# Attention and feed-forward kernel: lam fetched as one packet and spread over the partitions by a matmul, q and k first in SyncE's queue, one activation table for Ln and Exp, and a new order table for all engines

## The chip, the cores and the metric

One core of a Trainium2 chip runs the whole program. The metric is the time of one execution on the device in microseconds, as the median of several runs. Names of the engines: PE is TensorE (PEld its weight loads), DVE VectorE, ACT ScalarE, POOL GpSimd, SP SyncE, which here only starts DMAs. ACT and POOL start some DMAs too.

## The reference

Two steps, all inputs and the output in float32. The first is attention with a decay lam per head (batch 4, 8 heads, 768 positions, head size 64), in blocks of 64 positions with a running state. The second takes its result as 3072 tokens of 512 and puts them through two matrix products with a sine between them.

```python
rel = pos[:, None] - pos[None, :]
Dmask = np.where(rel >= 0, lam ** rel, 0.0)              # per head
for b in range(nb):                                      # blocks of 64 positions
    intra = (qb @ kb.T * Dmask) @ vb
    inter = (qb * lam ** (pos + 1)) @ kv_state
    out[b] = intra + inter
    kv_state = lam ** 64 * kv_state + (kb * lam ** (63 - pos)).T @ vb
x = out.transpose(0, 2, 1, 3).reshape(3072, 512)
h = x @ w_in                                             # 512 x 2048
g = h + np.sin(alpha * h) ** 2 / (alpha + 1e-9)
out = g @ w_out                                          # 2048 x 512
```

## The kernel before

**Attention** works on 24 blocks of 128 tokens (six to each batch). lam never enters a mask: q is multiplied by powers of lam (`Lq`), k by negative powers (`Lp` for the first four blocks, `Lk` for the rest), so that the scores need only a mask of zeros and ones. The powers are exp of n ln(lam): the exponents `E_f` come from iotas, `lnlam` is Ln of lam (L438), `lnL` the product of both (L441), and four exponentials (L443 to L449) make `Lq`, `Lp` and `Lk`. A block then goes: scaling of q and k on DVE or POOL (L468, L478, L485, L497), a cast of v (L491, L500), transposes on PE with copies to SBUF, scores (L618) and their masking into `Sm` on DVE (L629), the state `Z` (L654) with its casts `Zd` or `Zc` on ACT or DVE, and the output (L700 to L722; the first four blocks use L765 and L785), which is cast into `xT`, the transposed input of the feed-forward part (L732, L745).

**The feed-forward part** works on six chunks of 512 tokens. `unit_A` is 128 of the 2048 columns of h for 512 tokens: four matmuls into one PSUM bank (L828), the sine on ACT (L838), its square on ACT or POOL (L842, L843), and the sum with h on DVE (L845), which gives `gT` and frees the bank. `unit_A2` is the same work for two times 128 columns and half the tokens (L862 to L880). `unit_B` is the second product for chunk 0 (L893), with a copy to `osb` (L907) and stores on ACT's queue (L913). Chunks 1 to 5 do the second product in a form with seven products instead of eight (`unit_P`, L981). It needs five sums of quarters of w2 for each of two halves of w2, made once (`weight_sums`, L936, ten operations on DVE or POOL; three of each five go into other buffers, two are made in place in `w2`), and sums of `gT` for each chunk (`token_sums`, L959, on POOL or DVE). `finish` puts the products together (L1003 to L1027).

**The order.** `_Plan` collects about 1050 operations with what they read and write. A table, `ORDER`, holds for each engine the numbers of its operations in the order in which it issues them; where an operation may run on more than one engine, the table that lists its number decides. `emit` adds the semaphore waits. Each engine works through its list strictly in order: what waits holds all that stands behind it. DMAs are operations in these lists as well (`load`, L324), so a DMA holds its place on SP, ACT or POOL. Pairs in PE's table, such as (64, 128), are 64 filler matmuls of 128 columns on a buffer of ones (`spin`, L1140) that keep PE running while nothing else is ready.

**The start.** lam was loaded with a DMA that writes the same eight numbers to all 128 partitions (128 packets of 32 bytes), first in SP's queue, followed by k and q of the first four blocks, their v, and `ws`, the first 512 columns of w1 in float32, which ACT casts in two halves (L393). ACT loads three tables of functions: one for Ln (L438), one for Exp (brought in by a small operation, L440) and one for Sin (L450).

## Time and profile before

| | |
|---|---|
| time, median of 3 runs | 210.52 us (209.93 to 210.64) |
| profiled execution | 209.95 us |
| its span (first to last instruction) | 208.2 us |
| busy: PE, DVE, ACT, POOL | 200.0, 168.5, 147.7, 132.4 us |
| first matmul of the feed-forward part | 19.04 us after the span's start |
| granted TensorE clock | 1.00 from 19.2 to 180 us |

All times of the profile are microseconds from the start of the span. A row of the timeline gives start, duration, engine, line and operation, and in brackets the idle time ahead of it with what ended it. A row of the stretches gives its bounds, its length, PE's busy time with the number of instructions, the granted clock (1.00 is full), the share of the DMA engines and GB/s. A row of the DMA issues ends with KB and the median time from issue to landing.

### The profile page before, as it was taken

The numbers are of one execution on the slowest core, as the hardware profiler recorded it, in microseconds if no ns is written. First come the engines' busy times: TensorE is split into PE (matmuls) and PEld (weight loads), VectorE is DVE, ScalarE is ACT, GpSimd is POOL, SyncE is SP. The second block draws the span as 40 slices with busy tenths as digits, with TensorE's granted clock in tenths as the row PEclk, the third lists the DMA queues.
The fourth block names the chain that finished last, engine by engine and source line by source line (L and its number), as shares of the span: only waits on it lengthen the run. The fifth ranks groups of instructions, "written<-read, shape, count | busy, mean of one in ns | idle before, by whom it ended". The sixth has DMA issues, their size and how long they took to land.

```text
span 208.2 us, 4897 instructions
## 1 busy us (share of the span) xinstructions
PE 200.0 (96%) x1972; PEld 136.8 (66%) x1972; DVE 168.5 (81%) x296; ACT 147.7 (71%) x270; POOL 132.4 (64%) x140
## 2 busy tenths in 40 slices
PE   6988999999997999998999999999999999999995
PEld 6756444557765877665657576665667666667994
DVE  2898567886989999987988979899798866767854
ACT  5658999448998999976979776898765579734300
POOL 6065689834968987954796850958851695585400
DMA  4999999999899999799997999380300004000324
GB/s 133 323 315 216 202 255 214 213 238 245 197 179 230 232 250 248 154 215 206 208 245 156 242 271 185 67 194 26 136 0 3 0 32 169 3 0 20 128 94 165
DMA packets 83222, 34.40 MB, mean 165 GB/s; under 512 B 59632, under 2 KB 80384, under 8 KB 83200
## 3 DMA queue, kind: packets, MB, share of 16 engines
q1 hardware_dynamic: 78544, 29.24, 62.5%
q0 software_dynamic: 3696, 3.67, 10.9%
q10 hardware_dynamic: 960, 1.19, 1.9%
q8 instruction: 15, 0.25, 0.5%
q14 instruction: 7, 0.06, 0.1%
HBM read 27.28 MB, written 6.29 MB: 161 GB/s over the span
## 4 chain that ended last, share of the span: by engine, by line
PE 79%; DVE 9%; ACT 4%; DMA 3%; SPq 2%; issue 1%; ACTq 1%; POOL 0%
PE bank L828 28%; PE bank L981 26%; PE bank L862 7%; PE bank L893 6%; PE bank L722 3%; PE bank L618 3%; DMA v<-in_v_dram 3%; SPq L324 2%; DVE gT L880 2%; DVE Sm L629 2%; DVE gT L845 2%; PE bank L700 1%; DVE w L936 1%; PE bank L654 1%; ACT Zd L672 1%; PE bank L662 1%
## 5 line engine op out<-in xcount | busy, mean ns | idle before, releaser
L828 PE MATMUL bank<-xT,w 128*128 128x512 bf16 x296 | 70.9, 380 | 1.0 <-ACT kept L1018 0.7
L845 DVE SCALAR_TENSOR_TENSOR gT<-u,rinv,bank 128x512 bf16<-128x512 bf16 x74 | 53.6, 744 | 18.2 <-ACT u L842 14.1
L838 ACT ACTIVATE t<-bank,alpha 128x512 bf16<-128x512 f32 x74 | 49.9, 683 | 19.9 <-PE bank L828 19.0
L828 PEld LDWEIGHTS bank<-xT,w 128*128 128x128 bf16 x296 | 27.8, 98 | 28.8 <-DVE gT L845 1.4
L959 POOL TENSOR_TENSOR gT<-gT 128x512 bf16<-128x512 bf16 x28 | 32.1, 1158 | 14.1 <-DVE Xs L959 8.9
L842 ACT ACTIVATE u<-t 128x512 bf16<-128x512 bf16 x57 | 35.2, 628 | 1.5
L843 POOL TENSOR_TENSOR u<-t 128x512 bf16<-128x512 bf16 x17 | 17.6, 1040 | 25.7 <-ACT t L838 25.7
L629 DVE TENSOR_TENSOR Sm<-bank,mask 128x1024 bf16<-128x1024 f32 x24 | 28.9, 1216 | 3.0 <-PE bank L618 1.1
L862 PE MATMUL bank<-xT,w 128*128 128x256 bf16 x176 | 21.6, 273 | 1.0 <-DVE gT L880 1.0
L880 DVE SCALAR_TENSOR_TENSOR gT<-u,rinv,bank 128x256 bf16<-128x256 bf16 x44 | 18.9, 474 | 4.2 <-ACT u L876 3.5
L959 POOL TENSOR_TENSOR Xs<-gT 128x512 bf16<-128x512 bf16 x19 | 21.8, 1162 | 0.3 <-DVE gT L845 0.3
L981 PE MATMUL bank<-w,gT 128*128 128x256 bf16 (+1 forms) x168 | 20.1, 268 | 0.0
L872 ACT ACTIVATE t<-bank,alpha 128x256 bf16<-128x256 f32 x44 | 18.5, 471 | 2.0 <-PE bank L862 1.7
L981 PE MATMUL bank<-ws,gT 128*128 128x256 bf16 x160 | 19.6, 273 | 0.0
L981 PE MATMUL bank<-w,Xs 128*128 128x256 bf16 (+1 forms) x168 | 19.5, 268 | 0.0
L478 POOL TENSOR_TENSOR qk<-q,Lq 128x512 bf16<-128x512 f32 x17 | 18.2, 1077 | 2.0 <-DMA q<-in_q_dram 2.0
L497 POOL TENSOR_TENSOR qk<-k,Lk 128x512 bf16<-128x512 f32 x16 | 17.4, 1090 | 3.3 <-DMA k<-in_k_dram 3.2
L862 PEld LDWEIGHTS bank<-xT,w 128*128 128x128 bf16 x176 | 16.3, 98 | 4.2 <-DVE gT L880 1.8
L981 PEld LDWEIGHTS bank<-w,gT 128*128 128x128 bf16 x168 | 15.9, 98 | 4.1 <-DVE gT L959 0.2
L981 PEld LDWEIGHTS bank<-w,Xs 128*128 128x128 bf16 x168 | 15.6, 98 | 3.3
L981 PEld LDWEIGHTS bank<-ws,gT 128*128 128x128 bf16 x160 | 15.3, 98 | 3.1 <-ACT xT L732 0.4
L893 PE MATMUL bank<-w,gT 128*128 128x512 bf16 x64 | 15.8, 380 | 0.0
(105 smaller groups left out, 266.0 us busy)
## 6 DMA issues: line engine op xcount, KB each, us to landing
k<-in_k_dram SPq DMA_DIRECT2D x24, 256.0 KB, 5.1
q<-in_q_dram SPq DMA_DIRECT2D x12, 512.0 KB, 6.2
v<-in_v_dram SPq DMA_DIRECT2D x24, 256.0 KB, 5.8
out_dram<-osb SPq DMA_DIRECT2D x18, 256.0 KB, 2.6
w<-in_moe_w_out_dram POOLq DMA_DIRECT2D x4, 512.0 KB, 7.8
w<-in_moe_w_in_dram POOLq DMA_DIRECT2D x3, 512.0 KB, 8.1
ws<-in_moe_w_in_dram SPq DMA_DIRECT2D x2, 512.0 KB, 7.5
out_dram<-osb ACTq DMA_DIRECT2D x8, 128.0 KB, 3.7
```

Source lines behind the costliest of these rows:

```text
L478: lambda e, a=a: e.tensor_tensor(qk2[:, j:j + 2, 4 * a:4 * a + 4, :], q32[:, jq, 4 * a:4 * a + 4, :, :].rearrange("p h t d -> p t h d"), b ...
L629: op("DVE", lambda e: e.tensor_tensor(Sm[js][:, :, :], banks[:, 512 * b0:512 * b0 + 1024].rearrange("p (c i) -> p c i", i=128), bass.AP(ma ...
L828: ins = e.matmul(ps[hb][:, c0:c1], w1[:, kc, 128 * m:128 * (m + 1)], xT[x][:, kc, c0:c1], start=(kc == 0 and c0 == lo), stop=(kc == NKC - ...
L838: op("ACT", lambda e: e.activation(t16[ju][:, w], ps[hb][:, w], ACTF.Sin, scale=alpha[:, m:m + 1]), 0.69 if hi - lo == TCH else 0.475, [ba ...
L842: lambda e: (e.activation(u16[ju][:, w], t16[ju][:, w], ACTF.Square) if e is nc.scalar else e.tensor_tensor(u16[ju][:, w], t16[ju][:, w], ...
L845: op("DVE", lambda e: e.scalar_tensor_tensor(out=gT[g][:, m, w], in0=u16[ju][:, w], scalar=rinv[:, m:m + 1], in1=ps[hb][:, w], op0=ALU.mul ...
L862: ins = e.matmul(ps[hb][:, 256 * i:256 * i + 256], w1[:, kc, 128 * (m + i):128 * (m + i + 1)], xT[x][:, kc, lo:lo + 256], start=(kc == 0 a ...
L872: op("ACT", lambda e, i=i: e.activation(t16[ju][:, 256 * i:256 * i + 256], ps[hb][:, 256 * i:256 * i + 256], ACTF.Sin, scale=alpha[:, m + ...
L880: op("DVE", lambda e, i=i: e.scalar_tensor_tensor(out=gT[g][:, m + i, lo:lo + 256], in0=u16[ju][:, 256 * i:256 * i + 256], scalar=rinv[:, ...
L893: ins = e.matmul(ps[ob][:, w], gT[g][:, m, 128 * s4:128 * (s4 + 1)], w2[:, m, w], start=(m == 0), stop=(m == NM - 1),)
L959: e.tensor_tensor(dst, in0, in1, alu), 0, rd, wr))
L981: ins = e.matmul(ps[ob][:, lo + d0:lo + d1], lhs, rhs[:, d0:d1], start=first and p == 0, stop=(p == NM // 2 - 1), skip_group_check=True)
```

## The change

**lam.** It is loaded as one packet of eight numbers onto partition 0, on ACT's queue, ahead of alpha. Ln works on these eight numbers. A float32 matmul of a row of 128 ones with them writes the result to all 128 partitions of PSUM bank 7, where `lnL` reads it. The memset of the ones is a new DVE operation, the matmul a new PE operation behind the first 24 fillers (before, 64 fillers stood in one row).

**The tables.** ACT asks for one table that holds both Ln and Exp, right behind alpha's DMA. The small Exp operation (L440) is gone, and with it a table load; the Sin table is brought in as before.

```diff
-            load(lam_bc[:, :], bass.AP(lam.tensor, 0, [[0, 128], [1, H]]), "lam", 0.1, "lam", "SP", lat=0.8, runs=1)
-            load(alphaT[:, :], bass.AP(moe_alpha.tensor, 0, [[128, NM], [1, 128]]), "alphaT", 0.1, "alphaT", "ACT", lat=2.0, runs=1)
+            load(lam_sb[:, :], bass.AP(lam.tensor, 0, [[H, 1], [1, H]]), "lam", 0.1, "lam", "ACT", lat=0.8, runs=1)
+            def load_alpha(e):
+                ins = e.dma_start(alphaT[:, :], bass.AP(moe_alpha.tensor, 0, [[128, NM], [1, 128]]))
+                e.preload_act_table_set("natural_log_exp_and_others")
+                return ins
...
-            op("ACT", lambda e: e.activation(lnlam[:, :], lam_bc[:, :], ACTF.Ln), 0.25, ["lam"], ["lnlam"])
-            lnlam_b = bass.AP(lnlam, 0, [[H, 128], [0, 2 * NB + 4], [1, H]])
-            op("ACT", lambda e: e.activation(warm[:, :], lnlam[:, 0:1], ACTF.Exp, scale=0.0), 1.5, ["lnlam"], ["warm"])
+            op("DVE", lambda e: e.memset(ones[:, :], 1.0), 0.1, writes=["ones"])
+            op("ACT", lambda e: e.activation(lnlam[:, :], lam_sb[:, :], ACTF.Ln), 0.25, ["lam"], ["lnlam"])
+            op("PE", lambda e: e.matmul(ps[7][:, 0:H], ones[:, :], lnlam[:, :]), 0.3, ["ones", "lnlam"], [bank(7)])
+            lnlam_b = bass.AP(banks, 512 * 7, [[8 * 512, 128], [0, 2 * NB + 4], [1, H]])
...
-                        wr = [("T", i, x) for x in m] + ([("ws", 256 * (i // 3))] if i < 4 else [] if i == 4 else keys)
+                        wr = [("T", i, x) for x in m] + ([("ws", 0), ("ws", 256)] if i < 4 else [] if i == 4 else keys)
...
         "PE": (
-            (64, 128), 58, (5, 512), 60, 54, (11, 128), 38, 56, 52, 61, 66, 64, (1, 128), 68, 69, 74, 77,
+            (24, 128), 32, (5, 512), (33, 128), 57, 39, 59, 61, 53, 55, 62, (4, 512), 67, 65, 75, 69, 70, 82,
```

The line with `ws` makes the sums that are written into the buffer `ws` wait for both halves of w1's first cast.

**The order table** is new as a whole. The lists keep much of their shape; some 130 operations changed engine. POOL's list now has a scaling of k and one cast of v behind the last k, then a memset of `Zd`, and only then the loads of w1 and w2 (before: the scaling of k, three casts of v, then three loads of w1). The first half of w1's cast has moved from ACT to DVE. DVE has eight of the ten sums of w2 (before seven), POOL two (before three). Three places, line numbers of each kernel's own code:

SP's list at its start; `q32`, `k32`, `v32` are the float32 buffers of q, k and v, `ws` that of w1's first columns. Before:

```order
L324 DMA lam_bc<-in_lam_dram 128x8
L324 DMA k32<-in_k_dram 128x4x128
L324 DMA q32<-in_q_dram 128x4x256
L324 DMA k32<-in_k_dram 128x4x128
L324 DMA q32<-in_q_dram 128x4x256
L324 DMA k32<-in_k_dram 128x4x128 x2
L324 DMA v32<-in_v_dram 128x4x128 x4
```

SP's list at its start, of the changed kernel:

```order
L326 DMA q32<-in_q_dram 128x4x256 x2
L326 DMA k32<-in_k_dram 128x4x128 x2
L326 DMA v32<-in_v_dram 128x4x128
L326 DMA k32<-in_k_dram 128x4x128
L326 DMA v32<-in_v_dram 128x4x128
L326 DMA k32<-in_k_dram 128x4x128
L326 DMA v32<-in_v_dram 128x4x128 x2
```

lam's load is gone from this queue, both q stand ahead of all k, and the last k is now the eighth load, behind two v; it was the sixth data load.

ACT's list at its start, from alpha's load to the Sin table (`warm` is the small buffer of the operations that bring a table in). Before:

```order
L324 DMA alphaT<-in_moe_alpha_dram 16x128
L438 ACT_TABLE_LOAD
L438 ACTIVATE lnlam<-lam_bc 128x8
L440 ACT_TABLE_LOAD
L440 ACTIVATE warm<-lnlam 128x1
L445 ACTIVATE Lp<-lnL 128x32
L449 ACTIVATE Lq<-lnL 128x48
L447 ACTIVATE Lk<-lnL 128x48
L443 ACTIVATE Lq<-lnL 128x32
L450 ACT_TABLE_LOAD
```

ACT's list at the same place, of the changed kernel:

```order
L326 DMA lam_sb<-in_lam_dram 1x8
L409 DMA alphaT<-in_moe_alpha_dram 16x128
L410 ACT_TABLE_LOAD
L447 ACTIVATE lnlam<-lam_sb 1x8
L456 ACTIVATE Lk<-lnL 128x48
L452 ACTIVATE Lq<-lnL 128x32
L454 ACTIVATE Lp<-lnL 128x32
L458 ACTIVATE Lq<-lnL 128x48
L459 ACT_TABLE_LOAD
```

One table load and one operation are gone, lam's load stands here, and the exponentials have another order: `Lk` first, `Lp` third.

DVE's list around the sums of w2 that are made in place, in the first half of chunk 1 (`gT_1` is chunk 1's buffer, `u16` the squared sine, `rinv` 1/alpha, `bank` PSUM). Before:

```order
L936 TENSOR_TENSOR w2<-w2 128x4x256
L880 SCALAR_TENSOR_TENSOR gT_1<-u16_1,rinv,bank 128x256
L880 SCALAR_TENSOR_TENSOR gT_1<-u16_3,rinv,bank 128x256 x2
L880 SCALAR_TENSOR_TENSOR gT_1<-u16_1,rinv,bank 128x256
L936 TENSOR_TENSOR w2<-w2 128x4x256 x2
L880 SCALAR_TENSOR_TENSOR gT_1<-u16_1,rinv,bank 128x256 x2
L629 TENSOR_TENSOR Sm_0<-bank,mask_2 128x1024
```

DVE's list at that place, of the changed kernel:

```order
L945 TENSOR_TENSOR w2<-w2 128x4x256
L889 SCALAR_TENSOR_TENSOR gT_1<-u16_3,rinv,bank 128x256 x2
L889 SCALAR_TENSOR_TENSOR gT_1<-u16_1,rinv,bank 128x256
L916 COPY osb_1<-bank 128x512
L945 TENSOR_TENSOR w2<-w2 128x4x256
L889 SCALAR_TENSOR_TENSOR gT_1<-u16_1,rinv,bank 128x256 x2
L638 TENSOR_TENSOR Sm_0<-bank,mask_2 128x1024
```

Of three sums in place on DVE two are left, and no two stand next to each other; a copy to `osb` stands here now. In ACT's list the two stores of `osb_1` that stood next to each other now stand singly.

More of the change, by code (lines that the diff above doesn't have):

```diff
@@ L293, in bass_lightning_attn__then__act_snake_kernel @@
         identf = sb("identf", [128, 128], F32)
-        lam_bc = sb("lam_bc", [128, H], F32)
-        lnlam = sb("lnlam", [128, H], F32)
+        lam_sb = sb("lam_sb", [1, H], F32)
+        lnlam = sb("lnlam", [1, H], F32)
+        ones = sb("ones", [1, 128], F32)
         E_i = sb("E_i", [128, 2 * NB + 4, H], I32)
@@ L403, in _ @@
             last = {}
-            load(lam_bc[:, :], bass.AP(lam.tensor, 0, [[0, 128], [1, H]]), "lam", 0.1, "lam", "SP", lat=0.8, runs=1)
-            load(alphaT[:, :], bass.AP(moe_alpha.tensor, 0, [[128, NM], [1, 128]]), "alphaT", 0.1, "alphaT", "ACT", lat=2.0, runs=1)
+            load(lam_sb[:, :], bass.AP(lam.tensor, 0, [[H, 1], [1, H]]), "lam", 0.1, "lam", "ACT", lat=0.8, runs=1)
[3 more added lines that the diff above has]
+                return ins
+            op("ACT", load_alpha, 0.1, dma="alphaT", lat=2.0, issue=0.55, runs=1, writes=["alphaT"])
             load_q(0)
```

14 lines of the change are left out of this document (7 added, 7 removed), and 107 rows, old and new, of the table ORDER.

## The prediction

> **What bounds the kernel now.** I read the page first (busy shares and the chain that ended last), then PE's busy time by stretches, then the timeline up to the first matmul of the feed-forward part.
>
> ```profile
> span 208.2 us, 4897 instructions
> PE 200.0 (96%) x1972; PEld 136.8 (66%) x1972; DVE 168.5 (81%) x296; ACT 147.7 (71%) x270; POOL 132.4 (64%) x140
> ...
> DVE  2898567886989999987988979899798866767854
> ...
> PE 79%; DVE 9%; ACT 4%; DMA 3%; SPq 2%; issue 1%; ACTq 1%; POOL 0%
> ...
> 19.20:98.00 78.80, 76.88 (x737) 1.00 1.12 217
> 98.00:180.00 82.00, 81.85 (x720) 1.00 0.55 127
> ...
> 19.04 1.91 PE L862 MATMUL bank<-xT,w 128*128 128x256 bf16 x16
> ```
>
> The reader is to see that TensorE holds 79% of the chain, and that from 98 us to 180 us it is idle for 0.15 us in all. In the row of the stretch from 19.2 us to 98 us it is idle for 78.80 - 76.88 = 1.92 us. The row of digits is VectorE's busy share in 40 slices of 5.2 us each: it is at 90% or more in five slices in a row, from 62 to 88 us. The first row of the feed-forward part (the last line) starts at 19.04 us. The change removes no matmul behind that point, so the end can move for two reasons only: the first such matmul starts at another time, or the 1.92 + 0.15 = 2.07 us of idle time behind it become less or more.
>
> Where those 1.92 us lie is told by two rows of PE's timeline (in brackets the wait ahead of the row and what ended it):
>
> ```profile
> 65.21 1.05 PE L862 MATMUL bank<-xT,w 128*128 128x256 bf16 x8 [0.97 <-DVE gT L880]
> 98.08 1.04 PE L828 MATMUL bank<-xT,w 128*128 128x512 bf16 x4 [0.73 <-ACT kept L1018]
> ```
>
> Together 1.70 of the 1.92 us. The first is the queue of VectorE: the gT that frees the bank stands behind two sums of w2. The last is ScalarE's queue, which had been held while it issued two stores:
>
> ```profile
> 62.24 2.13 DVE L936 TENSOR_TENSOR w<-w 128x1024 bf16<-128x1024 bf16 x2
> 62.22 1.60 POOL L497 TENSOR_TENSOR qk<-k,Lk 128x512 bf16<-128x512 f32 x1
> 93.77 1.66 ACTq L913 DMA_DIRECT2D out_dram<-osb  x2
> ```
>
> **The change, part by part: SyncE's queue.** These are the issues and landings that count (the times behind the sizes are from issue to landing):
>
> ```profile
> 0.81 0.40 SPq L324 DMA_DIRECT2D lam_bc<-in_lam_dram  x1
> 1.25 0.42 SPq L324 DMA_DIRECT2D k<-in_k_dram  x1
> 4.19 0.93 SPq L324 DMA_DIRECT2D k<-in_k_dram  x1
> ...
> k<-in_k_dram SPq DMA_DIRECT2D x1, 256.0 KB, 3.6
> k<-in_k_dram SPq DMA_DIRECT2D x1, 256.0 KB, 6.4
> ...
> 6.35 6.02 DMA v<-in_v_dram
> ...
> 14.53 0.61 POOL L491 CAST v<-v 128x512 bf16<-128x512 f32 x1 [1.50 <-DMA v<-in_v_dram]
> 15.89 0.62 ACT L491 CAST v<-v 128x512 bf16<-128x512 f32 x1
> ```
>
> lam's slot on SyncE goes, so every load behind it is issued 1.25 - 0.81 = 0.44 us earlier. What the stream itself gains lies between nothing (if the transfers and not the issues set the landings) and the 1.05 us between lam's landing (0.81 + 3.0) and the first k's (1.25 + 3.6); I take 0.44, the slot. The first k landed at 4.85, the sixth load (the last k, issued 4.19) at 10.6, the eighth (the second v) at 6.35 + 6.02 = 12.37, and the last v between 14.5, when POOL got the third, and 15.9, when ScalarE cast it. In the new order the last k is the eighth load instead of the sixth. The first eight carry 2.5 MB either way, so it lands at 12.37 - 0.44 = 11.9 us, **1.3 us later than now**, the first two v land one to two us earlier, and the last v between 14.1 and 15.4; I take 14.8.
>
> **lam, its Ln and the tables.**
>
> ```profile
> 1.66 5.60 PE L1140 MATMUL bank<-Xs 128*128 128x128 bf16 x64 [1.66 <-DVE Xs L419]
> 4.09 1.28 ACT L440 ACT_TABLE_LOAD   x1
> 4.11 0.29 DVE L441 TENSOR_TENSOR lnL<-E_f,lnlam 128x128 f32<-128x128 f32 x1 [2.36 <-ACT lnlam L438]
> 5.68 0.23 ACT L445 ACTIVATE Lp<-lnL 128x32 f32<-128x32 f32 x1
> 5.95 0.69 DVE L485 TENSOR_TENSOR qk<-k,Lp 128x512 bf16<-128x512 f32 x1 [1.41 <-ACT Lp L445]
> 9.90 0.23 PE L453 MATMUL bank<-identf,alphaT 16*128 16x16 f32 x1
> ```
>
> The matmul with ones stands behind 24 fillers, and one filler takes 5.60 / 64 = 87 ns: 1.66 + 24 x 0.087 = 3.75 us. Its own cost is not shown; the other float32 matmul of this size (L453) takes 0.23, and between nothing and twice that the sum does not move. So lnL begins near 4.1 us, where it begins now: spreading Ln by a matmul gains nothing by itself. The second table load (1.28) goes, and the exponentials begin at about 4.45 instead of 5.68 us. The 1.41 us that VectorE waits for Lp go with it. What is late next is the data: the first q is 512 KB and lands between the first two loads of now, at about 5.2 us. VectorE's scalings begin some 0.7 us earlier than 5.95.
>
> **From there to the first feed-forward matmul.** The rows for the walk:
>
> ```profile
> 10.74 1.04 POOL L485 TENSOR_TENSOR qk<-k,Lp 128x512 bf16<-128x512 f32 x1 [5.46 <-DMA k<-in_k_dram]
> 11.72 0.64 PE L618 MATMUL bank<-qkT 64*64 64x128 bf16 x32 [0.70 <-ACT qkT L544]
> 12.18 4.62 DVE L629 TENSOR_TENSOR Sm<-bank,mask 128x1024 bf16<-128x1024 f32 x4 [0.37 <-PE bank L618]
> 12.36 0.61 PE L566 MATMUL bank<-ident,qk 128*128 128x128 bf16 x8
> 13.00 1.07 ACT L577 COPY qkT<-bank 128x512 bf16<-128x512 bf16 x2 [1.43 <-PE bank L566]
> 16.72 1.34 DVE L745 CAST xT<-bank 128x512 bf16<-128x512 f32 x2
> 16.93 1.05 ACT L393 CAST w<-ws 128x1024 bf16<-128x1024 f32 x1
> 16.95 0.62 PE L654 MATMUL bank<-v,qk 64*128 64x128 bf16 x8 [0.47 <-ACT Zd L672]
> 18.00 0.76 ACT L672 CAST Zd<-bank 64x256 bf16<-64x256 f32 x2
> 18.81 0.40 PE L785 MATMUL bank<-qkT,Zd 128*128 128x128 bf16 x4 [0.34 <-ACT Zd L672]
> ...
> 15.09 2.43 POOL L324 DMA_DIRECT2D w<-in_moe_w_in_dram  x3
> 99.26 0.42 DVE L500 CAST v<-v 128x512 bf16<-128x512 f32 x1
> ```
>
> The first score matmuls, now at 11.72, come at about 11.1, since the scalings are 0.6 us ahead. VectorE's first two of four Sm (4.62 / 4 = 1.15 each) then run from 11.5 to 13.8. The last k, at 11.9, takes POOL 1.04 (to 12.95), its transposes 0.61 (13.5), ScalarE's two copies 1.07 (14.6), and the third Sm can start near 14.4, on the first copy. Two Sm end at 16.7, about where all four end now (12.18 + 4.62 = 16.80). Behind them VectorE has one xT (1.34 / 2 = 0.67, to 17.4) and the first half of w1, which moves here from ScalarE: not shown there, bounded by twice the nearest row, 0.42, and by ScalarE's 1.05; I take 0.8, to 18.2. Beside it ScalarE casts both last v (0.62 each, 14.8 to 16.1); the state update on TensorE takes 0.62 (16.7), its two Zd 0.76 (17.4, no longer behind the w1 cast that held them from 16.93 to 18.00), and two pieces with Zd 0.40 each (18.2). **The first feed-forward matmul moves from 19.04 to about 18.2: 0.84 us gained.** The ends: 1.8 us if the late k costs nothing, and a loss of 0.6 if that k, POOL's scaling and the copies each come some 0.5 us later than I count. The second half of w1 (ScalarE, 1.05) is needed only after the first two units, 1.91 us together in the first row of the feed-forward part quoted above, and is hidden by them; should ws land over 0.5 us later than I count, it shows in full. POOL now waits for the last k, and a Zd memset and the w1 and w2 loads are queued behind that wait: POOL issues them near 13.5 instead of 15.09, since it has one v cast instead of three, so units 4 to 15 have their weights no later than now.
>
> **Behind 19 us.** The new search keeps PE's order nearly as it is. VectorE gets eight of the ten w2 sums instead of seven, six of them early; the two in place now stand apart with gT between them, as the order shows; ScalarE's stores of osb_1 stand singly. So both causes of the two big waits are loosened. I cannot derive new waits from rows, so I bound: at most the 2.07 us can be won; a loss has its price in the rival below. Of 2.07 I take 0.6, less than the one wait of 0.97, because VectorE is at 90% or more there and what is pulled out of one place is put into another. Tail and epilogue are the same instructions in nearly the same order: nothing.
>
> The profiled run took 209.95 us, its span 208.2 and 1.75 around it; 209.95 - 0.84 - 0.6 = 208.5. The median of the three runs, 210.52, lies 0.57 above that run, so the forecast is 210.52 - 1.44 = **209.1 us**.
>
> **One rule against it.** Three sums of w2 on VectorE differ:
>
> ```profile
> L936 DVE TENSOR_TENSOR w<-w x3: 685/687/1532, 60.0 to 62.8; 128x1024 bf16<-128x1024 bf16 x3
> L936 POOL TENSOR_TENSOR w<-w x1: 2126/2126/2126, 68.0 to 68.0; 128x1024 bf16<-128x1024 bf16 x1
> ```
>
> The slow one took 1532 - 685 = 847 ns more, in just the stretch in which POOL ran L497 (62.22 to 63.82), and it is the one ahead of PE's 0.97 us. The Trainium skill, "SBUF — State Buffer", section "Who interferes with whom", says that a VectorE instruction with both inputs in SBUF and a GpSimd instruction that reads SBUF exclude each other for a whole instruction; by that rule the 847 ns are the rest of POOL's instruction, which the trace agrees with.
>
> **The rivals.** (1) *VectorE held by POOL, the other side.* POOL now holds two in-place w2 sums in a row (2.13 each), and VectorE's own two, and its token sums, come around the same time. Each meeting costs VectorE the 0.85 seen, up to a whole 2.13. VectorE is full from 62 to 88 us, so it shows in full once the slack in front of a gT is used up. Three meetings cost 2.5; with the start gained that is 210.52 - 0.84 + 2.5 = 212.2. It decides from two meetings on. For it: the 1532. Against it: one such meeting among three sums now. By the skill's rule alone every overlap would cost; my chance is weighed from one in three: 0.14. (2) *New waits as large as the gain.* The start moves, and VectorE's early sums, which stand ahead of the last gT of chunk 0 and wait for a w2 load, hand 0.9 us back: 210.5, chance 0.16. For it: VectorE's five full slices. (3) *The start doesn't move*, because the last k is two places later and nothing else waits: 19.0 to 19.6 at the first feed-forward matmul, 209.9 to 211.4 in all, chance 0.10, half of it within 0.3%. That lam's new way does nothing for lnL is part of the forecast already.
>
> **The numbers.** A measurement here tells about 0.3%, 0.63 us, from no change. The forecast has 0.60, with a range of its own of 207.8 to 209.8 (from all idle time won, to nothing won behind a start 0.7 earlier). Faster 0.60; within 0.3%: 0.16 + 0.05 = 0.21; slower 0.14 + 0.05 = 0.19. The range reaches from 207.8 up into rival (3) at 211.2, and leaves out rival (1) and the best case.
>
> **What will show it.** Right: the first feed-forward matmul at about 18.2 us; exponentials near 4.5; lnL still near 4.1; the last k waited for by POOL near 11.9; PE's idle time up to 98 us below 1.9. Wrong: a first feed-forward matmul at 19 or later, VectorE sums of over 1 us with POOL beside them, or a wait of PE over 1 us that these rows don't have.

## The result, and the profile after

| | before | changed |
|---|---|---|
| median, beside each other on one chip | 210.33 us (209.93 to 211.51, 6 runs) | **213.28 us** (211.72 to 215.66, 6 runs) |
| ratio, with its 95% interval | | **1.012** (1.0076 to 1.0164): slower |
| profiled execution, its span | 209.95, 208.2 us | 211.72, 209.9 us |
| first matmul of the feed-forward part | 19.04 us | 18.56 us |
| PE idle, 19.2 to 98 us | 1.92 us | 3.87 us |
| PE idle, 98 to 180 us | 0.15 us | 0.03 us |

The forecast was 209.1 us with a range of 207.8 to 211.2; the time lies outside the range, and the change is slower instead of faster. Ratios and their intervals leave out disturbed runs (the traces of w2_early and all_three below are of such runs), medians take all runs. The profiled execution is the fastest of the six: the medians differ by 2.95 us, the two profiled executions by 1.77, so about 1.2 us of the loss are not in the two traces.

The page's head, the two stretches, and PE's timeline of the changed kernel (its lines are those of before plus nine in the body):

```profile
span 209.9 us, 4870 instructions
PE 199.9 (95%) x1957; PEld 135.3 (64%) x1957; DVE 167.9 (80%) x296; ACT 153.4 (73%) x279; POOL 123.0 (59%) x130
...
PE 69%; DMA 18%; DVE 7%; SPq 2%; POOL 2%; issue 0%; ACT 0%
...
19.20:98.00 78.80, 74.93 (x715) 1.00 1.10 215
98.00:180.00 82.00, 81.97 (x735) 1.00 0.56 127
...
18.56 2.04 PE L871 MATMUL bank<-xT,w 128*128 128x256 bf16 x16
40.23 1.04 PE L902 MATMUL bank<-w,gT 128*128 128x512 bf16 x4 [0.72 <-DMA w<-in_moe_w_out_dram]
47.29 0.40 PE L709 MATMUL bank<-qkT,Zd 128*128 128x128 bf16 x4 [0.90 <-DVE Sm L638]
53.19 0.40 PE L525 MATMUL bank<-ident,qk 128*128 128x128 bf16 x4 [1.08 <-DVE qkT L558]
53.97 1.05 PE L871 MATMUL bank<-xT,w 128*128 128x256 bf16 x8 [0.38 <-DVE gT L889]
65.15 1.91 PE L871 MATMUL bank<-xT,w 128*128 128x256 bf16 x16
90.85 1.05 PE L990 MATMUL bank<-w,Xs 128*128 128x256 bf16 x8 [0.51 <-DVE osb L1036]
```

DMA holds 18% of the chain instead of 3%. The span's 1.7 us split into -0.48 at the start, +1.95 up to 98 us and -0.12 behind it; some 0.35 is left over. The two big waits of before are gone: the row at 65.15 has no bracket, and there is none over 0.2 us at 98. Four new ones between 40 and 54 us make 0.72 + 0.90 + 1.08 + 0.38 = **3.08 us**. Cut at 60 us, the stretch shows it too (bounds, length, then busy time of PE, PEld, DVE, ACT and POOL); first the kernel before, idle there for 0.01 us:

```profile
19.20:60.00 40.80, 40.79 (x337) 23.73 (x334) 30.76 (x53) 32.50 (x63) 30.22 (x31) 1.00 1.19 223
```

and the changed kernel, with 3.09:

```profile
19.20:60.00 40.80, 37.71 (x294) 20.80 (x292) 32.74 (x53) 29.89 (x57) 22.02 (x24) 1.00 1.14 220
```

The wait at 40.23 is for a w2 load issued at 30.88. Loads of w2 took longer than before, by the list of DMA issues from 20 to 45 us (the last number is the median time to landing), before and changed:

```profile
w<-in_moe_w_out_dram POOLq DMA_DIRECT2D x4, 512.0 KB, 7.8
```

```profile
w<-in_moe_w_out_dram POOLq DMA_DIRECT2D x3, 512.0 KB, 9.3
```

Of the third load alone: before, it was issued at 31.18 us and landed 8.4 us later, at 39.6; now it is issued at 30.88 and lands 9.3 us later, at 40.2. VectorE's list shows where the other three come from:

```profile
43.96 2.14 DVE L945 TENSOR_TENSOR ws<-w 128x1024 bf16<-128x1024 bf16 x2 [0.42 <-DMA w<-in_moe_w_out_dram]
46.02 1.21 DVE L638 TENSOR_TENSOR Sm<-bank,mask 128x1024 bf16<-128x1024 f32 x1
48.35 2.12 DVE L487 TENSOR_TENSOR qk<-q,Lq 128x512 bf16<-128x512 f32 x2
51.01 1.52 DVE L506 TENSOR_TENSOR qk<-k,Lk 128x512 bf16<-128x512 f32 x1
52.45 0.68 DVE L558 COPY qkT<-bank 128x1024 bf16<-128x1024 bf16 x1
```

Two early w2 sums wait for a w2 load, and behind them stand the Sm and the qkT copy that PE wants. They are slow besides: a pair of the same sums took 1.27 us at 37.58.

The last new wait, at 90.85, is small here, but has a mechanism that the prediction does not hold. Rows of ScalarE's stores and VectorE's subtractions, and the page's row of the stores:

```profile
85.61 0.54 ACTq L922 DMA_DIRECT2D out_dram<-osb  x1
90.10 0.69 DVE L1036 TENSOR_TENSOR osb<-bank,kept 128x512 f32<-128x512 f32 x1 [1.28 <-DMA out_dram<-osb]
103.31 0.69 DVE L1036 TENSOR_TENSOR osb<-bank,kept 128x512 f32<-128x512 f32 x1 [0.19 <-DMA out_dram<-osb]
...
85.61 4.46 DMA out_dram<-osb
...
out_dram<-osb ACTq DMA_DIRECT2D x8, 128.0 KB, 4.1
```

The store issued at 85.61 takes 4.46 us to land, and VectorE is free for the subtraction that overwrites its `osb` after 90.10 - 1.28 - 85.61 = 3.2 us.

### The profile page after: what moved, and what is told of

Same layout as the page of the kernel before. It is cut to its first block, busy times and chain, and to the rows that moved or that the text cites. A ratio compares the mean times of both kernels' runs of the same rounds, so it can differ in the third digit from the quotient of the medians.

```text
span 209.9 us, 4870 instructions
## 1 busy us (share of the span) xinstructions
PE 199.9 (95%) x1957; PEld 135.3 (64%) x1957; DVE 167.9 (80%) x296; ACT 153.4 (73%) x279; POOL 123.0 (59%) x130
## 4 chain that ended last, share of the span: by engine, by line
PE 69%; DMA 18%; DVE 7%; SPq 2%; POOL 2%; issue 0%; ACT 0%
PE bank L990 29%; PE bank L837 24%; PE bank L871 6%; DMA w<-in_moe_w_out_dram 5%; DMA w<-in_moe_w_in_dram 4%; DMA q<-in_q_dram 3%; PE bank L731 3%; DMA k<-in_k_dram 3%; PE bank L627 3%; SPq L326 2%; DMA out_dram<-osb 2%; PE bank L902 2%; DVE Sm L638 1%; PE bank L709 1%; DVE ws L945 1%; DVE qk L487 1%
## 5 line engine op out<-in xcount | busy, mean ns | idle before, releaser
L851 ACT ACTIVATE u<-t 128x512 bf16<-128x512 bf16 x64 | 39.8, 629 | 1.9
L968 POOL TENSOR_TENSOR gT<-gT 128x512 bf16<-128x512 bf16 x27 | 30.9, 1153 | 13.6 <-DVE gT L854 6.8
L968 POOL TENSOR_TENSOR Xs<-gT 128x512 bf16<-128x512 bf16 x23 | 26.4, 1154 | 12.5 <-DVE gT L854 12.5
L506 POOL TENSOR_TENSOR qk<-k,Lk 128x512 bf16<-128x512 f32 x16 | 16.9, 1068 | 6.5 <-DMA k<-in_k_dram 5.3
L990 PE MATMUL bank<-w,Xs 128*128 128x256 bf16 (+1 forms) x168 | 20.0, 268 | 0.5 <-DVE osb L1036 0.5
L881 ACT ACTIVATE t<-bank,alpha 128x256 bf16<-128x256 f32 x44 | 18.2, 471 | 2.8 <-PE bank L871 2.7
L852 POOL TENSOR_TENSOR u<-t 128x512 bf16<-128x512 bf16 x10 | 10.3, 1039 | 15.1 <-ACT t L847 13.3
L741 ACT CAST xT<-bank 128x512 bf16<-128x512 f32 x15 | 11.0, 733 | 9.2 <-PE bank L663 4.6
```

What stands on the lines that cost most here:

```text
L506: lambda e: e.tensor_tensor(qk2[:, j, H:2 * H, :], block32(k32, jl), lk, ALU.mult), 1.05,
L851: lambda e: (e.activation(u16[ju][:, w], t16[ju][:, w], ACTF.Square) if e is nc.scalar else e.tensor_tensor(u16[ju][:, w], t16[ju][:, w], ...
L881: op("ACT", lambda e, i=i: e.activation(t16[ju][:, 256 * i:256 * i + 256], ps[hb][:, 256 * i:256 * i + 256], ACTF.Sin, scale=alpha[:, m + ...
L968: e.tensor_tensor(dst, in0, in1, alu), 0, rd, wr))
L990: ins = e.matmul(ps[ob][:, lo + d0:lo + d1], lhs, rhs[:, d0:d1], start=first and p == 0, stop=(p == NM // 2 - 1), skip_group_check=True)
```

## The experiments

The theories: **D**, a w2 load near 40 us sets the pace, so that an earlier start is handed back; **Q**, VectorE's list (its early sums and its meetings with GpSimd) costs the time; **W**, stores that land too late hold VectorE's overwrites; **T**, the loads share one stream, so that a w2 load pulled ahead makes k late; **F**, the start is set by the clock's warm-up and the columns of fillers ahead of the first transposes, not by lam; **G**, short idle gaps of PE bring the clock down. All kernels compute the whole reference; they differ in the order table, except that the pieces of before and of the changed code are mixed where it says so. Diffs show pieces of the table: the numbers are those of the operations. In some kernels the line numbers are some lines smaller than the changed kernel's (L1032 for L1036).

| kernel | median us | ratio to before (95%) |
|---|---|---|
| start_only | 210.99 | 1.0027 (0.9999 to 1.0054) |
| rest_only | 211.39 | 1.0053 (1.0031 to 1.0075) |
| lam_only | 211.02 | 1.0005 (0.9971 to 1.0039) |
| sums_late | 212.84 | 1.0141 (1.0102 to 1.0180) |
| relief | 212.96 | 1.0108 (1.0068 to 1.0149) |
| stores_early | 211.22 | 1.0013 (0.9969 to 1.0057) |
| before_stores_late | 209.57 | 0.9957 (0.9933 to 0.9982) |
| w2_early | 214.08 | 1.0042 (0.9996 to 1.0088) |
| start_w2 | 212.98 | 1.0104 (1.0057 to 1.0150) |
| all_three | 210.72 | 0.9974 (0.9935 to 1.0013) |
| stores_relief | 211.03 | 1.0018 (0.9995 to 1.0042) |
| stores_relief_w2c | 209.06 | 0.9924 (0.9897 to 0.9951) |
| stores_fill8 | 212.44 | 1.0088 (1.0061 to 1.0115) |
| w2c_nofill | **208.64** | **0.9910** (0.9875 to 0.9946) |
| w2c_gapfill | 209.32 | 0.9944 (0.9915 to 0.9973) |
| w2c_kfirst | 210.91 | 0.9994 (0.9956 to 1.0033) |

### The start alone, the rest alone, lam alone

**start_only** is the changed code with its lists up to the first feed-forward matmul, and the order and engines of before behind it. POOL's piece:

```diff
-... 29, 102, 103, 105, 104, 127, 149, 138, 161,
+... 29, 102, 103, 104, 199, 133, 105, 142, 149,
```

> The changed code with its own lists up to the first feed-forward matmul, and behind that the order and the engines of the kernel before. Theory Q (the loss is VectorE's list between 37 and 53 us, where sums of w2, copies to osb and scalings stand ahead of what PE waits for): the start gain of 0.5 us stays, first feed-forward matmul near 18.6 us, 209.8 us. Rival D (the w2 loads set the pace, so what PE gains at the start it waits for at unit_B): first feed-forward matmul near 18.6 us, but PE then waits about 0.6 us for a w2 load near 40 us, 210.3 us. If the start itself were the cause of the loss: 213 us.

The first feed-forward matmul came at 18.42 us, and the time did not fall. One row of PE:

```profile
38.16 1.90 PE L899 MATMUL bank<-w,gT 128*128 128x512 bf16 x8 [1.74 <-DMA w<-in_moe_w_out_dram]
```

The wait for the w2 load is larger than the start's gain. D holds for this half, and more than D says: this load was issued at 28.46 us and took 9.7 us to land, at 38.16; before, it was issued at 28.96 and took 7.3, to 36.3. So the data came 1.9 us later. Why the same load took longer is not shown.

**rest_only** is the other half, before's code and lists up to there.

```diff
-            (24, 128), 32, (5, 512), (33, 128), 57, 39, ...
+            (64, 128), 58, (5, 512), 60, 54, (11, 128), 38, ...
```

> The kernel before with its own lam, tables and lists up to the first feed-forward matmul, and behind that the order and the engines of the changed kernel. Theory Q: first feed-forward matmul near 19.0 us, the two waits behind VectorE (0.9 for Sm, 1.1 for qkT) as in the changed kernel, 213.2 us or a little more. Rival D: with the later start the wait for w2 shrinks from 0.7 to 0.2 us, and most of the loss goes: 211.3 us.

Slower by 0.5% with the old start (19.11 us). PE waits 1.48 us for the w2 load at 41.57, and VectorE twice for stores, 1.34 and 0.44 us. The time is the one expected under D (211.3), but not for D's reason: the wait for w2 did not shrink with the later start, it grew. Neither half gains, and their 0.27% and 0.53% together lie at the lower end of the whole change's interval.

**lam_only** is before with nothing but lam's new way (packet, matmul, one table).

```diff
-            (64, 128), 58, (5, 512), 60, 54, (11, 128), 38, ...
+            (24, 128), 32, (40, 128), 59, (5, 512), 61, 55, (11, 128), 39, ...
```

> The kernel before with the new way of lam alone: one packet on ScalarE's queue, the matmul behind the first 24 of the 64 fillers, one table for Ln and Exp; all lists otherwise as before. Theory F (PE's fillers and the matmul of 0.6 us stand ahead of the first transposes): lnL begins near 5.1 instead of 4.1 us, the first transposes at 8.0 to 9.0, 0.5 us later than before, the loads land 0.4 us earlier, and the two cancel: 210.4 us. Rival: the table load that is gone shows, first feed-forward matmul near 18.4 us, 209.8 us.

No change: 1.0005. `lnL` came at 5.09 us instead of 4.11, the first transposes at 8.34, the first feed-forward matmul at 19.93. lam's new way by itself gains nothing, as F has it. Nor did the later start of this trace (19.93 against 19.04) lengthen the time.

### VectorE's list

**sums_late** puts three early sums of w2 behind later operations of VectorE.

```diff
-... 200, 331, 332, 222, 246, 238, 211, 260, 333, 213, 251, 257, 256, 259, 270, 269, 272, 280, 278, 277, 288, 289, ...
+... 200, 222, 246, 238, 211, 260, 213, 251, 257, 256, 259, 331, 270, 269, 332, 272, 280, 278, 277, 288, 289, 333, ...
```

> The changed kernel with VectorE's three sums of the second half of w2 moved behind the first gT of chunk 1 (two of them from 44 us to about 51 and 52 us, the third from 50 to about 54 us). Theory Q: PE's wait of 0.9 us for Sm goes, and that of 1.1 us for qkT is at most 0.3; 211.7 us. Rival D: no change, 213.2 us. Rival P (VectorE and POOL hold each other up, wherever the sums stand): the sums take over 1 us each at their new place too and PE waits there, 213 us.

The waits for Sm at 47 and for qkT at 53 were gone, and the time stayed at 1.014. Other waits stood in their place:

```profile
59.68 0.41 PE L719 MATMUL bank<-qkT,Zc 64*64 64x128 bf16 x8 [0.96 <-DVE Sm L635]
47.36 1.28 DVE L484 TENSOR_TENSOR qk<-q,Lq 128x512 bf16<-128x512 f32 x2
```

The second row is a reading by the way: the two scalings of q, 2.12 us in the changed kernel with POOL's L506 beside them from 48.58, took 1.28 here, where POOL was idle from 45.9 to 48.75. So in these rows the slow VectorE instructions are those that meet POOL's. The Trainium skill, "SBUF — State Buffer", section "Who interferes with whom", has the rule of the two excluding each other; these rows agree with it.

**relief** takes work off VectorE instead: two copies to `osb` go to ScalarE, one scaling of q to POOL.

```diff
  ACT
-... 225, 224, 227, ...
+... 225, 224, 246, 238, 227, ...
  DVE
-... 222, 246, 238, 211, 260, 333, 213, ...
+... 222, 211, 333, 213, ...
  POOL
-... 27, 212, 219, ...
+... 27, 212, 260, 219, ...
```

> The changed kernel with two copies to osb moved from VectorE to ScalarE, which is idle at 46 us, and one scaling of q from VectorE to POOL, which is idle at 45.6 us; the sums of w2 stay in place. Theory Q: VectorE's list from 47 to 52 us is 2.3 us shorter, the wait of 1.1 us for qkT goes, that of 0.9 us for Sm stays; 212.1 us. Rival D: 213.2 us. Rival P: POOL's extra scaling slows VectorE's sums, and at most 0.5 us is won.

No gain either: 1.0108. But its trace showed the stores at full size, on VectorE, on PE behind it and in the chain:

```profile
104.51 0.69 DVE L1032 TENSOR_TENSOR osb<-bank,kept 128x512 f32<-128x512 f32 x1 [2.15 <-DMA out_dram<-osb]
105.92 1.04 PE L833 MATMUL bank<-xT,w 128*128 128x512 bf16 x3 [1.99 <-DVE gT L850]
...
98.50 5.93 DMA out_dram<-osb
```

A store took 5.93 us to land, VectorE stood for 2.15 us in front of the overwrite, and the gT behind it came 1.99 us late for PE. Q alone does not explain the time; from here W was a theory of its own.

### The stores

**stores_early** changes nothing but the places of the eight stores in ScalarE's list.

```diff
-... 390, 392, 387, 377, 376, 378, 417, 416, 397, 396, 407, 398, 244, 373, 410, 411, 412, 427, 240, 451, ...
+... 390, 392, 244, 387, 377, 376, 378, 240, 417, 416, 397, 396, 407, 398, 243, 373, 410, 411, 412, 427, 239, 451, ...
```

> The changed kernel with ScalarE's eight stores of chunk 0 issued earlier in its list (the last store of osb_0 and osb_1 from 85.6 to about 77 us, the last of osb_2 and osb_3 from 99.3 to about 91 us). Theory W (VectorE may overwrite osb only when chunk 0's stores have landed, and the new list issues them up to 10 us later than before): VectorE's waits for stores at 90 us (1.28) and 103 us (0.2 to 2.2 from run to run) go, and PE's waits of 0.5 and up to 2.0 us behind them; 212.0 us, with less spread. Rivals Q and D (VectorE's list at 44 to 53 us, the w2 loads) alone: no change, 213.2 us.

From 1.012 to 1.0013, with intervals that do not touch: **about 1.1% of time came from where the stores stand**. Between 80 and 112 us no instruction of VectorE waited for a store any more (a wait of 0.81 us at 202 us, 0.94 in the changed kernel, is for stores of the tail); PE's waits of 1.02 us (w2, at 41.40), 0.90 (Sm) and 0.89 (qkT) were still there. W holds. The same eight places are the whole difference between relief (1.0108) and stores_relief (1.0018) below, again with intervals that do not touch; their traces have the same start (first feed-forward matmul at 19.41 and 19.42 us), and PE's waits of 0.89 us at 90.08 and 1.99 us at 105.92 are gone in the second.

**before_stores_late** is the reverse on the kernel before: its stores go later in ScalarE's list and stand singly.

```diff
-... 410, 409, 239, 411, 238, 426, 372, 450, 451, 242, 452, ...
+... 410, 409, 411, 426, 239, 372, 450, 451, 452, ...
```

> The kernel before with ScalarE's last seven stores of chunk 0 moved in its list to the places that the changed kernel gives them, and nothing else. Theory W: VectorE waits over 1 us for a store ahead of a subtraction into osb, once near 87 to 90 us and once near 101 us, and PE 0.5 to 2 us behind each; 211.9 us. Rival: the places of the stores matter only beside the changed kernel's other lists; no change, 210.4 us.

It became faster, 0.9957. The expectation of a loss failed, and its rows say why:

```profile
88.16 0.69 DVE L1027 TENSOR_TENSOR osb<-bank,kept 128x512 f32<-128x512 f32 x1
98.13 1.03 PE L828 MATMUL bank<-xT,w 128*128 128x512 bf16 x4
...
84.15 3.72 DMA out_dram<-osb
```

The subtraction at 88.16 does not wait (nor does the other, at 101.89): it comes 4.0 us behind its store, which took 3.72. And PE's 0.73 us at 98 are gone with the pair of stores that had held ScalarE, in a trace that began the feed-forward part at 19.68 us, 0.64 later than before's. So a later store is not bad in itself; what counts is the distance from its issue to the overwrite, which the changed kernel cut to 3.2 us while landing took 4.46.

### The loads of w2

**w2_early** pulls three of POOL's w2 loads ahead in the changed kernel.

```diff
-... 104, 127, 149, 138, 161, 153, 106, 196, 107, 195, 108, 199, 197, 27, ...
+... 104, 127, 106, 149, 138, 161, 153, 107, 108, 196, 195, 199, 197, 27, ...
```

> The changed kernel with POOL's last three loads of w2 issued earlier in its list (from 28.4, 30.9 and 32.7 us to about 22, 28.4 and 29.2 us). Theory D (w2 sets the pace of unit_B near 40 us): PE's wait of 0.7 to 1.2 us for w2 goes, 212.3 us. Rival T (the transfers of that stretch fill the DMA engines, so what w2 gains q, k and v lose): the wait moves to the transposes of blocks 4 and 5, near 35 us, or to VectorE's scalings near 48 us, 213.2 us.

The loads of w2 were early, and k was late. PE's row, and stretches of the same trace:

```profile
43.18 0.58 PE L522 MATMUL bank<-ident,qk 128*128 128x128 bf16 x4 [4.45 <-POOL qk L503]
...
38.70:43.20 4.50, 0.06 (x2) 0.88 0.77 177
43.20:46.00 2.80, 2.70 (x12) 0.50 1.19 306
```

PE waited 4.45 us for k's scaling (two loads of k landed 13.7 and 16.5 us after their issue; 7.6 and 7.7 in the changed kernel), and then the granted clock, third from the right, was at 0.50 in the next stretch. The trace supports T, the loads share one stream, but the ratio of 1.0042 is not that of this execution (span 219.2 us): it says only that three loads pulled ahead leave no gain over the kernel before, and not how long k's wait usually is.

**start_w2** does the same to start_only.

```diff
-... 133, 105, 142, 149, 161, 165, 27, 106, 157, 107, 196, ...
+... 133, 105, 106, 142, 149, 107, 161, 165, 108, 27, 157, 196, ...
```

> The kernel of start_only (new start, old order behind it) with the w2 loads issued earlier, directly behind the first one and between POOL's first squares. Theory D: the wait of 1.7 us for w2 near 37 us goes, what the start gained shows, 209.8 us. Rival T: the wait moves to the transposes or scalings of blocks 4 and 5, 210.9 us.

1.0104, against 1.0027 without it. In this trace PE's wait for w2 was 0.53 us (at 32.41) instead of 1.74, so the remedy did what it was meant for, and a load of k took 15.0 us to land instead of 7.8, as T has it, but PE waited only 0.20 us for it. What made the kernel slower is therefore not seen at these loads. Two things stand elsewhere: the first feed-forward matmul came at 19.45 us (18.42 in start_only), and the mean granted clock was between 0.984 and 0.992 in four of the six executions.

**all_three** is stores_early, w2_early and relief in one; POOL's and ScalarE's pieces:

```diff
-... 104, 127, 149, 138, 161, 153, 106, 196, 107, 195, 108, 199, 197, 27, 212, 219, ...
+... 104, 127, 106, 149, 138, 161, 153, 107, 108, 196, 195, 199, 197, 27, 212, 260, 219, ...
-... 225, 224, 227, ...
+... 225, 224, 246, 238, 227, ...
```

> The changed kernel with the earlier stores, the earlier w2 loads, two copies to osb on ScalarE and one scaling of q on POOL. If W, D and Q each hold a part of the loss: 213.2 - 1.2 - 0.9 - 0.7 = 210.4 us, as the kernel before, with the start's 0.5 us making up for what is left of the waits. If one cause of them is wrong: 211.3 us or more.

0.9974, not told apart from before. In its trace PE waited 3.89 us for k at 42.27, with the clock at 0.57 for 3.7 us behind it: the picture of w2_early again, and with the same reserve.

**stores_relief** is stores_early and relief, without the loads. Against stores_early:

```diff
-... 225, 224, 227, ...
+... 225, 224, 246, 238, 227, ...
-... 27, 212, 219, ...
+... 27, 212, 260, 219, ...
```

> The changed kernel with the earlier stores, and two copies to osb on ScalarE and one scaling of q on POOL instead of VectorE. Theory Q on top of W: with the stores out of the way, the shorter list of VectorE shows, PE's waits of 0.9 for Sm and 0.9 for qkT become 0.4 in all; 1.2 us less than with the earlier stores alone, 209.8 us. Rival D: the w2 load near 40 us and the data behind it pace PE there, no more than 0.3 us is won, 210.8 us.

1.0018, not told apart from stores_early's 1.0013. The waits for Sm and qkT were gone from the trace, with one of 1.12 us for w2 left. So Q's waits are real, but removing them moves PE only up to that load: what they cost of the total is not shown.

**stores_relief_w2c** adds one swap in POOL's list: the third w2 load stands right behind the second.

```diff
-            106, 196, 107, 195, 108, 199, 197, 27, 212, 260, ...
+            106, 107, 196, 195, 108, 199, 197, 27, 212, 260, ...
```

> The kernel with the earlier stores and the shorter list of VectorE, and the third load of w2 issued right behind the second, ahead of a scaling that waits for q (from 30.9 to 29.2 us); the second and fourth keep their places. Theory D: the wait of 0.7 to 1.0 us for that load near 40 us shrinks by up to 0.8 us without pushing k behind it; 209.2 us. Rival T: what w2 gains, k or v lose, as with all w2 loads early; 209.8 us or, with a long wait of PE near 40 us, more.

0.9924, the first that beats before. The wait for w2 is almost gone:

```profile
39.48 1.04 PE L902 MATMUL bank<-w,gT 128*128 128x512 bf16 x4 [0.19 <-DMA w<-in_moe_w_out_dram]
```

The kernel gains 0.9% on stores_relief, but not all of it can be the load's. PE's wait for w2 went from 1.12 us to 0.19, which is 0.4% of the time. The trace of stores_relief also began the feed-forward part 1.08 us later (19.42 us against 18.34) and ran its first 16 matmuls at a lower clock, in 3.49 us instead of 2.04; both stand ahead of the swapped load, which is issued behind 28 us, and cannot come from it. So D's wait is shown, and its remedy works where one load moves a little; its share of the 0.9% is not settled.

### The fillers and the clock

**stores_fill8** is stores_early with lam's matmul behind 8 fillers instead of 24, so that `lnL` is not held by PE.

```diff
-            (24, 128), 32, (5, 512), (33, 128), 57, ...
+            (8, 128), 32, (16, 128), (5, 512), (33, 128), 57, ...
```

> The changed kernel with the earlier stores, and 8 filler matmuls ahead of the one that spreads Ln instead of 24 (the other 16 stand behind it). Theory L (the late k and v loads set the start, not lnL): lnL begins 0.9 us earlier, near 4.1 us, the first feed-forward matmul stays near 18.6 us; as with the earlier stores alone, 211.0 us. Rival: lnL holds the scalings and so the start; the first feed-forward matmul comes 0.5 us earlier, 210.5 us.

Slower, 1.0088 against 1.0013. PE's rows from lam's matmul on:

```profile
3.33 0.59 PE L448 MATMUL bank<-lnlam,ones 1*128 1x8 f32 x2 [0.50 <-ACT lnlam L447]
3.85 5.63 PE L1149 MATMUL bank<-Xs 128*128 128x128 bf16 x54
9.32 0.39 PE L548 MATMUL bank<-ident,qk 128*128 128x128 bf16 x4
```

`lnL` was over a microsecond earlier (3.95 us), but behind the idle 0.50 us in front of lam's matmul the 54 fillers took 5.63 us, and the first transposes came at 9.32 us (8.81 in stores_early, 8.20 in the changed kernel). That the idle time kept the fillers slow is inferred from these rows. The first feed-forward matmul came at 20.01 us, later than either theory had it.

**w2c_nofill** is stores_relief_w2c without the five wide fillers.

```diff
-            (24, 128), 32, (5, 512), (33, 128), 57, ...
+            (24, 128), 32, (33, 128), 57, ...
```

> The kernel of stores_relief_w2c without the 5 fillers of 512 columns that the new list of PE has ahead of the first transposes. Theory F: the first transposes come at 7.3 to 7.9 instead of 8.2 us or later, the first feed-forward matmul 0.4 us earlier on average, 208.5 us. Theory L (the last k and v set the first feed-forward matmul): it stays near 18.4 us, 208.8 us. Theory G (PE idle in the start lets the granted clock drop at 19 us): more runs below full clock, 209.5 us.

The best kernel, 0.9910, with the narrowest runs (208.45 to 208.99):

```profile
span 206.8 us, 4858 instructions
...
7.77 0.40 PE L548 MATMUL bank<-ident,qk 128*128 128x128 bf16 x4 [0.79 <-DVE qk L477]
18.31 2.04 PE L871 MATMUL bank<-xT,w 128*128 128x256 bf16 x16
...
18.40:98.00 79.60, 78.34 (x743) 1.00 1.16 225
```

Now the first transposes wait for data (0.79 us for the scaled q), not for fillers, at 7.77 us; up to 98 us PE is idle for 1.26 us. The first feed-forward matmul stays where it was in the trace of stores_relief_w2c (18.31 us against 18.34), as theory L has it and not F. The interval of the ratio overlaps that of stores_relief_w2c, so the share of the wide fillers in the total is not settled.

**w2c_gapfill** adds three wide fillers in two gaps of the start, against G; they ran at 16.31 and 18.78 us.

```diff
-... 80, 85, 87, 90, 93, 91, ...
+... 80, 85, (2, 512), 87, 90, (1, 512), 93, 91, ...
```

> The kernel of stores_relief_w2c with 3 fillers of 512 columns in PE's two waits between 15.7 and 18.2 us. Theory G: the runs with a granted clock below 0.995, about one in four with the new start so far, vanish; the time of the others stays at 208.8 us or is up to 0.2 us more. If PE's idle time there has no part in it, the share stays at one in four.

0.9944, no better, and its trace had the clock at 0.51 from 14.6 to 18 us all the same, from before the first of these fillers. G is not supported.

**w2c_kfirst** puts k and q as pairs and k ahead of v in SP's list.

```diff
-... 4, 5, 8, 6, 9, 7, 10, 11, ...
+... 4, 5, 6, 7, 8, 9, 10, 11, ...
```

> The kernel of stores_relief_w2c with all loads of k ahead of those of v on SyncE's queue, so that the last k is the sixth load again. Theory L: POOL's scaling of the last k begins near 10.3 instead of 11.9 us, the third and fourth Sm follow each other without the wait of 0.95 us, the first feed-forward matmul comes up to 0.9 us earlier unless v holds it, 208.2 us. Rival: v, which lands up to 1.8 us later, takes the place of k; 18.4 us and 208.8 us.

Back to 0.9994. ScalarE's cast of v, which stands ahead of the copies of qkT, now waits for a later v, and PE for the copies:

```profile
12.19 0.81 PE L627 MATMUL bank<-qkT 64*64 64x128 bf16 x32 [1.27 <-ACT qkT L553]
20.71 1.58 PE L871 MATMUL bank<-xT,w 128*128 128x256 bf16 x7
...
12.20:18.50 6.30, 4.46 (x129) 1.00 1.08 253
18.50:22.00 3.50, 3.46 (x50) 0.52 1.23 203
```

The start's last 2 us are the lower clock's (0.52, third from the right) as well. The two v ahead of the last k, which the prediction counted as that k's loss, are what the lists behind them are made for.

## Why the prediction was wrong, step by step

**The start moves to 18.2: right in kind, half in size, and not in every execution.** The late k came as computed: POOL had it at 11.89 us (11.9 forecast), the third Sm began at 14.62 (14.4), and VectorE's half of w1 took 0.67 us (0.8) and ended at 18.18 (18.2). What came later is the other side, ScalarE's and TensorE's. The last casts of v ended at 16.32 us instead of 16.1, the state update behind them took 0.89 us instead of 0.62, and the pieces with Zd followed:

```profile
16.37 0.89 PE L663 MATMUL bank<-v,qk 64*128 64x128 bf16 x8 [0.63 <-ACT v L500]
17.29 0.76 ACT L681 CAST Zd<-bank 64x256 bf16<-64x256 f32 x2 [0.36 <-PE bank L663]
18.11 0.62 PE L794 MATMUL bank<-qkT,Zd 128*128 128x128 bf16 x8 [0.28 <-ACT Zd L681]
```

Between these two traces 0.48 us were gained, not 0.84. Over all traces the gain is not settled. In those with the changed start lists this state update begins at 16.36 to 16.45 us, and then they part: in relief, stores_early, start_w2 and stores_relief PE stands for 0.90 to 1.00 us in the middle of it, and the first feed-forward matmul comes at 19.41 to 19.45 us; in start_only, sums_late, all_three, stores_relief_w2c and w2c_nofill it comes at 18.31 to 18.74. The old lists had 19.04, 19.11 and 19.68 (before, rest_only, before_stores_late). The row of stores_early:

```profile
17.81 0.33 PE L660 MATMUL bank<-v,qk 64*128 64x128 bf16 x3 [0.90 <-issue]
```

"issue" means that the profile shows nothing that PE waited for. Among these traces the long gaps are in those whose first transposes came at 8.35 us or later, but what the gap is stays open.

The front was late as well, which the prediction did not have:

```profile
1.79 2.74 PE L1149 MATMUL bank<-Xs 128*128 128x128 bf16 x24 [1.79 <-DVE Xs L427]
4.47 0.59 PE L448 MATMUL bank<-lnlam,ones 1*128 1x8 f32 x2
4.99 3.37 PE L1149 MATMUL bank<-Xs 128*128 128x512 bf16 x38
5.10 0.29 DVE L450 TENSOR_TENSOR lnL<-E_f,bank 128x128 f32<-128x128 f32 x1 [2.47 <-PE bank L448]
8.20 0.39 PE L548 MATMUL bank<-ident,qk 128*128 128x128 bf16 x4
```

I took one filler at 5.60 / 64 = 87 ns, a mean over a row whose first part is slow: the 24 took 2.74 us, 114 ns each, and lam's matmul 0.59 instead of about 0.23. `lnL` came at 5.10 us, not 4.1, and the exponentials at 5.42, not 4.45. The Trainium skill, "TensorE: Matmul & The Clock Gate", section "Part 1: The HAM clock gate", tells of a warm-up at half rate; the slower first fillers agree with it, though the profile's row of the granted clock shows full speed there. Also not counted: the changed list has 24 x 128 + 5 x 512 + 33 x 128 = 9856 columns of fillers ahead of the first transposes, where before had 64 x 128 = 8192. Up to 16.4 us this cost nothing: first transposes at 7.77 us (w2c_nofill) and at 8.81 (stores_early) were followed by that state update at 16.39 and 16.45.

**The start's gain reaches the end: wrong.** The prediction carried 0.84 us to the end as a matter of course. The w2 loads near 40 us take it: start_only is not faster, with 1.74 us of PE's wait there, and the traces of before_stores_late and lam_only, which began the feed-forward part 0.64 and 0.89 us later than before's, belong to kernels that are faster and the same. Rival (2) named this load, for the sums alone and with 0.9 us; the second product waits for it as well, and 3.08 us of new waits stood in the trace.

**"So both causes of the two big waits are loosened", and 0.6 us won behind the start: the step that failed.** The two waits did go, and before_stores_late shows that singly placed stores are worth 0.43%, as that step had it. But I looked at a store only as something that holds ScalarE's queue. I did not ask who waits for it to land: VectorE's overwrite of the same `osb`. That costs about 1.1% (stores_early against the changed kernel; 0.9% in the pair of relief and stores_relief), nearly the whole of the loss, though in the changed kernel's own trace it is only 1.28 + 0.19 us on VectorE and 0.51 on PE. In relief's it is 2.15 at one place. In place of the 0.6 us won, PE's idle time up to 98 us rose by 1.95 us.

**Rival (1), VectorE held by POOL**, came near the time (212.2) by a mechanism that is there: by rows (2.14 - 1.27) + (2.12 - 1.28) + (1.52 - 0.68) = 2.55 us more on VectorE, three meetings' worth. They are not the meetings that it named: the sums in place on VectorE took 0.68 us each at 63.14 and 65.96, undisturbed, and the slow rows are early sums and scalings beside POOL's scalings. And sums_late and relief, which take that load away, did not gain by themselves, so its share of the total is not shown. **Rival (3)**, a start that does not move, is not borne out by the changed kernel's trace (0.48 us), but its 19.0 to 19.6 us are seen in the four traces with the long gap, for a reason other than the late k.

**What stays open.** The intervals do not split the 1.2% exactly, and the parts do not add up simply: rest_only has the changed stores too, with waits of 1.34 and 0.44 us on VectorE, and is slower by only 0.5% in all. Some 1.6 us of the median are not in the changed kernel's trace. Two things could fill them, and neither is shown to: the stores, whose waits on PE were 0.89 and 1.99 us in relief's trace against 0.51 here, and PE's gap in the start, which this trace has only in part (0.89 - 0.62 = 0.27 us) and relief's in full (0.94). What the w2 load by itself is worth is open too, as said above.

## What to carry to other kernels

When a search moves a store, look at the operation that overwrites the stored buffer: the distance from issue to overwrite has to exceed the landing time under load (3.72, 4.46 and 5.93 us in the rows above). A gain at the start is worth what the arrival of the next loads leaves of it, so read the slack of the loads behind it before carrying it to the end. Pull one load at a time, and look at what then lands late. And take more than one trace of a start before its gain is counted: here the same lists gave 18.3 and 19.4 us.

## What the runs showed of the hardware

- **The warm-up is visible when fillers precede the work.** The first 24 fillers of 128 columns took 2.74 us, 114 ns each; the 33 behind lam's matmul in w2c_nofill took 2.02 us, 61 ns each. The same 38 fillers behind lam's matmul took 3.10 to 3.99 us from trace to trace (3.37 in the profile after), with the first transposes at 7.77 to 8.81 us.
- **The granted clock fell to about half** behind PE's idle time of 4 us (w2_early 0.50, all_three 0.57), but also in the start, near 15 to 23 us, behind stretches that were only partly idle (w2c_gapfill 0.51 from 14.6 to 18 us, with no gap of PE over 0.30 us between 8 us and there; w2c_kfirst 0.52 from 18.5 to 22, behind 4.46 us busy of 6.30). The same section of the Trainium skill tells of a return to half rate after an idle window; the first case agrees with it, and what sets off the second is open. It came with the new start: the mean granted clock of an execution was below 0.995 in 48 of 129 executions of the kernels with the changed start or a variant of it, and in 1 of 131 with the old start (before, rest_only, before_stores_late).
